# Strassen's seven block products in the output projection of an attention and SwiGLU kernel, with x in a ring of six batches

## The chip, the cores and the metric

The kernel runs on one core of a Trainium2 chip. The metric is device time in microseconds (us), the median of several runs; lower is better. The engines are TensorE (PE; its weight loads are shown as PEld), VectorE (DVE), ScalarE (ACT), GpSimd (POOL) and SyncE (SP, which issues DMAs here).

## What is computed

Attention with a decay per position, causal, for 8 batches of 8 heads with 576 positions of 64 numbers; its output, laid out as 4608 tokens of 512 numbers, goes through a SwiGLU block with a width of 1536. Inputs and output are float32.

```python
scores = scale * np.matmul(q, k.transpose(0, 1, 3, 2))
cum = np.cumsum(np.log(np.clip(f, 0.0001, 1.0)), axis=-1)
scores = np.where(causal, -1000000000.0, scores + cum[:, :, :, None] - cum[:, :, None, :])
attn = softmax(scores)                       # over the last axis
x = np.matmul(attn, v).transpose(0, 2, 1, 3).reshape(B * S, H * D)   # 4608 x 512
g = x @ w_gate                               # w_gate, w_val: 512 x 1536
out = (g * (1.0 / (1.0 + np.exp(-g))) * (x @ w_val)) @ w_out         # w_out: 1536 x 512
```

## The kernel before

All matrix products take bf16 operands and accumulate in float32 in PSUM, which is divided into eight banks of 128 x 512 float32: four in a pool "f" (the block's products), two in "s" (attention's scores), one in "o" (attention's output), one in "t" (transposes).

Attention goes by pairs of heads of a batch (`attention`, and `attention2` for batch 0). Scores (`score`, line 699) go to a bank, ACT takes the exponential (`expo`, line 733), POOL zeroes what is above the diagonal (`mask`, line 742), PE weighs the values (`weigh`, line 756), DVE divides by the sums (lines 763 and 768), and a transpose on PE or by DMA puts the result into `xT`, which holds x transposed for all 4608 tokens.

The block goes by nine tiles of 512 tokens (`ffn`). Twelve units per tile (`unit`), one for each 128 of the 1536 columns: PE computes the gate product in four matmuls (`gate`, line 901) into one bank and the value product into another; ACT takes tanh(g/2) (line 905), DVE adds 1 and multiplies by g (line 909), then by the value product (line 912), which gives twice the wanted result as a bf16 block in `HH` (16 buffers of 128 x 512). The output projection (`project`, line 916) then takes the tile in four blocks of 128 tokens: for each, twelve matmuls of 512 columns, with a block of `HH` as the weights and `wo` streaming, into one bank. ACT copies the bank to `OT` with a factor 0.5 (line 920), and SP stores 256 KB (line 923). For the very last block of tokens the 512 columns are cut at 256, 384 and 448.

The order of the instructions on each engine is fixed when the kernel is built. Operations are declared with a key, the operations they come after, the buffers that they take and a cost in us for each engine that may run them. A planner (`Plan.run`) simulates the engines with these costs: whenever an engine comes free, it issues the ready operation with the lowest key. Attention has keys from 1000 to some 9000, the block's PE work keys from 100000 up by tile, the block's ACT and DVE work -5 and -4. So on PE attention goes first whenever it is ready, and the block fills what is left. A table of keys for the first operations, `ORDER`, replaces their computed keys. On the chip each engine goes through its list in order and waits where an input is late.

Of the kernel before, what the change touches and what calls it, by code (L numbers as in the profile page):

```python
# [9 lines left out]
F32 = mybir.dt.float32  # L10
# [210 lines left out]
def kernel(ctx, tc, q, k, v, f, w_gate, w_val, w_out, out):  # L221
    nc = tc.nc
# [30 lines left out]
    def sb(name, shape, dt):  # L253
        return consts.tile(shape, dt, name=name)
# [23 lines left out]
    def ps(b):  # L278
        return bank[bank_of[b.pool] + b.i]
# [5 lines left out]
    flat = OT[1][:, :NFL]  # L285
    ones = OT[0].bitcast(BF16)[:BH, :S]
# [4 lines left out]
    zc, zt = HH[0][:, :384], HH[1][:, :384]  # L291
    QN = [[xT[:, r, c * S : (c + 2) * S].rearrange("p (u x) -> p u x", u=2) for r in range(KD)] for c in (6, 4)]

    plan = Plan(
        {"f": 4, "s": 2, "o": 1, "t": 1, "qk": NQK, "pt0": NPT0, "pt": NPT, "vb": NVB, "nv": NNV,
         "xn": NXN, "rc": NRC, "th": NTH, "hh": NHH, "ot": NOT},
        lambda t: 2.0 if t < TWARM else 1.0,
    )

# [21 lines left out]
    def copy(e, dst, src):  # L321
        if e == "ACT":
            nc.scalar.activation(dst, src, AF.Copy)
        else:
            E[e].tensor_copy(dst, src)  # L325
# [449 lines left out]
    def put(e, p, bt, qb, nq):  # L775
        b, r = divmod(p, FB)
        n = min(S, (qb + nq) * P) - qb * P
        copy(e, xT[:, r, b * S + qb * P : b * S + qb * P + n], ps(bt).bitcast(BF16)[:, :n])

    def cross(e, p, bx):  # L780

        b, r = divmod(p, FB)
        dst = xT[:, r, b * S : b * S + NB * P].rearrange("p (n t) -> p n t", t=P)
# [40 lines left out]
    def attention2(b, key, parts):  # L824

        bx = {}
        for n, (bks, qb, nq) in enumerate(parts):
            ahead = len(parts) > 1 and n == 0
            got = {}
            for jj in range(4):  # L830
# [21 lines left out]
                for u, h in enumerate(heads):  # L852
# [13 lines left out]
                    if len(prev) == 2:  # L866
                        x_out(b * FB + r, qb, nq, bx[n, r], prev, kk)

    def attention(p, key):
        b = p // FB  # L870
        bks, qb, nq = (0, 1, 2, 3), 0, NB
        bx, scaled = Buf("xn"), []
        for j in range(2):
            h = 2 * p + j
            bo, ws, x1 = Buf("o"), [], None
            for m, i in enumerate(bks):
                bs = Buf("s")
                a = op(("PE", mm(*[x[2] for x in BANKS[i]])), score, h, i, bs, after=q_ready[h] + [o_qkz], take=[bs], use=[hqk[p]],
                       key=key + 0.5 * j + 0.1 * i, tag=("s", h, i))
# [17 lines left out]
            nc.gpsimd.dma_start(out=t[:, :, lo:hi], in_=src[:, :, lo:hi])  # L897

    def gate(e, w, fc, t0, n, bf):
        for ko in range(KD):  # L900
            nc.tensor.matmul(ps(bf)[:, :n], w[:, ko, fc * P : (fc + 1) * P], xT[:, ko, t0 : t0 + n],  # L901
                             start=(ko == 0), stop=(ko == KD - 1))

    def tanh(e, n, bf, bt):
        nc.scalar.activation(TH[bt.i][:, :n], ps(bf)[:, :n], AF.Tanh, scale=0.5)  # L905
# [2 lines left out]
        t = TH[bt.i][:, :n]  # L908
        nc.vector.scalar_tensor_tensor(out=t, in0=t, scalar=1.0, in1=ps(bf)[:, :n], op0=ALU.add, op1=ALU.mult)  # L909

    def times(e, n, bf, bt, bh, lo):
        nc.vector.tensor_mul(HH[bh.i][:, lo : lo + n], TH[bt.i][:, :n], ps(bf)[:, :n])  # L912

    def project(e, hs, lo, m, bf, fcs, c):
        for fc in fcs:
            nc.tensor.matmul(ps(bf)[:m, c], HH[hs[fc].i][:, lo : lo + m], wo[:, fc, c],  # L916
                             start=(fc == 0), stop=(fc == KF - 1))

    def out_copy(e, m, bf, bo, c):
        nc.scalar.activation(OT[bo.i][:m, c], ps(bf)[:m, c], AF.Copy, scale=0.5)  # L920

    def store(e, t0, m, bo, c):
        E[e].dma_start(out=out[t0 : t0 + m, c], in_=OT[bo.i][:m, c])

    w_ready = {}
    last_gate = [None]

    def unit(t, fc, t0, n, hs, lo, kk, after):
        needs = [o for a, b, done in x_ready.values() if a < t0 + n and b > t0 for o in done]
        wr = [w_ready["g", fc // FCG], w_ready["v", fc // FCG]]  # L930
        bg, bv, bt = Buf("f"), Buf("f"), Buf("th")
        g = op(("PE", mm(*[n] * KD)), gate, wg, fc, t0, n, bg, after=needs + wr + after, take=[bg], key=kk, tag=("gp", t, fc))
# [3 lines left out]
        fresh = hs[fc] is None  # L936
        if fresh:
            hs[fc] = Buf("hh")
            hs[fc].first = None
        m = op(("DVE", dve(n)), times, n, bv, bt, hs[fc], lo, after=[a, b, hs[fc].first],  # L940
               take=[hs[fc]] if fresh else [], use=[bv, bt] + ([] if fresh else [hs[fc]]), key=-5, tag=("mul", t, fc))
        if fresh:
            hs[fc].first = m
        return g, m

    def ffn(t, t0, n):
        key, hs, ms = 1e5 * (t + 1), [None] * KF, []
# [7 lines left out]
        for m0 in range(0, n, P):  # L955
            m = min(P, n - m0)
            bo = Buf("ot")
            cuts = ENDS if t0 + m0 + m == N_TOK else [0, DM]
            for c in (slice(a, b) for a, b in zip(cuts, cuts[1:])):
                w, at = c.stop - c.start, m0 + c.start / DM  # L960
                bf = Buf("f")
                a = None
                for g in range(NCO):
                    fcs = range(g * FCO, (g + 1) * FCO)
                    a = op(("PE", mm(*[w] * FCO)), project, hs, m0, m, bf, fcs, c,
                           after=[m_ for fc in fcs for m_ in ms[fc]] + [w_ready["o", c] for c in range(NCO)] + [a],
                           take=[] if g else [bf], use=[hs[fc] for fc in fcs] + ([bf] if g else []),
                           key=key + 2000 + at + 0.01 * g, tag=("fo", t, m0))
                a = op(("ACT", act(w)), out_copy, m, bf, bo, c, after=[a] + (o_out2 + regrouped if t == 0 else []), take=[] if c.start else [bo],
                       use=[bf] + ([bo] if c.start else []), key=-4, tag=("ot", t, m0))  # L970
                last = len(cuts) > 2 and c.stop == DM
                op(("ACT", 0.45) if last else ("SP", 0.7), store, t0 + m0, m, bo, c, after=[a], use=[bo], key=-4, dma=w / DM, packet=90, tag=("out", t, m0))

    for g in range(2):
        four(g, -20 + 5 * g)
# [159 lines left out]
```

## Time and profile before

| | |
|---|---|
| median of 3 runs | 383.54 us (383.19 to 383.68) |
| span of the profiled execution, first to last instruction | 381.2 us |
| PE busy | 372.5 us (98%) |
| PEld busy | 208.4 us (55%) |
| DVE busy | 217.8 us (57%) |
| ACT busy | 213.1 us (56%) |
| POOL busy | 139.3 us (37%) |
| gate and value products, line 901 | 110.1 + 109.3 us busy |
| output projection, line 916 | 103.1 us busy |

The page gives no time of its own for the profiled execution besides its span; the runs' times include what surrounds the span. "Busy" is the time covered by an engine's recorded instructions; matmuls are pipelined and overlap one another in the record, so the time from the start of one group to that of the next tells more of PE than the duration of one instruction. In a group's row, the number before the bar is the count, then come its busy time, the mean duration in ns, and the idle time of the engine before it with what ended it. A row of stretches gives each engine's busy time in that stretch, with the number of instructions in brackets. A row of the timeline gives start and length, and in brackets the idle time before it.

### The profile page before, as it was taken

The numbers are of one execution on the slowest core, as the hardware profiler recorded it, in microseconds if no ns is written. First come the engines' busy times: TensorE is split into PE (matmuls) and PEld (weight loads), VectorE is DVE, ScalarE is ACT, GpSimd is POOL, SyncE is SP. The second block draws the span as 40 slices with busy tenths as digits, with TensorE's granted clock in tenths as the row PEclk, the third lists the DMA queues.
The fourth block names the chain that finished last, engine by engine and source line by source line (L and its number), as shares of the span: only waits on it lengthen the run. The fifth ranks groups of instructions, "written<-read, shape, count | busy, mean of one in ns | idle before, by whom it ended". The sixth has DMA issues, their size and how long they took to land.

```text
span 381.2 us, 8360 instructions
## 1 busy us (share of the span) xinstructions
PE 372.5 (98%) x3105; PEld 208.4 (55%) x3151; DVE 217.8 (57%) x456; ACT 213.1 (56%) x436; POOL 139.3 (37%) x368
## 2 busy tenths in 40 slices
PE   8899999999999999999999999999999999999996
PEld 5667656546555555545565456545664444444444
DVE  7878995377425771477327751586228815733850
ACT  7999745247647665646675467647773323323322
POOL 8897337117534454344353446603440000000000
PEclk9999999999999999999999999999999999999999
DMA  8999996996598788999499959993431011002003
GB/s 146 192 196 197 206 204 128 198 198 122 106 217 198 148 152 158 226 180 197 99 210 204 191 119 218 194 194 72 108 95 40 2 55 55 2 28 83 3 0 111
DMA packets 125319, 51.96 MB, mean 136 GB/s; under 512 B 112110, under 2 KB 119726, under 8 KB 124510
## 3 DMA queue, kind: packets, MB, share of 16 engines
q1 hardware_dynamic: 108782, 36.18, 45.0%
q0 software_dynamic: 16288, 15.14, 27.0%
q8 instruction: 24, 0.39, 0.4%
q14 instruction: 17, 0.14, 0.1%
q10 hardware_dynamic: 208, 0.11, 0.1%
HBM read 38.56 MB, written 17.07 MB: 146 GB/s over the span
## 4 chain that ended last, share of the span: by engine, by line
PE 94%; DMA 2%; ACT 1%; issue 1%; POOL 1%; DVE 0%; POOLq 0%
PE ps L901 48%; PE ps L916 24%; PE ps L699 10%; PE ps L756 8%; DMA xT<-in_k_dram 2%; PE ps L717 1%; ACT PT L733 1%; PE ps L773 1%; PE ps L574 0%; POOL xT L550 0%; PE ps L725 0%; PE ps L1004 0%; ACT PTa L733 0%; PE ps L558 0%; DVE QK L325 0%
## 5 line engine op out<-in xcount | busy, mean ns | idle before, releaser
L905 ACT ACTIVATE th<-ps 128x512 f32<-128x512 f32 (+1 forms) x112 | 65.0, 582 | 87.8 <-PE ps L901 85.3
L901 PE MATMUL ps<-xT,wv 128*128 128x512 bf16 (+1 forms) x435 | 110.1, 371 | 0.7
L909 DVE SCALAR_TENSOR_TENSOR th<-th,ps 128x512 f32<-128x512 f32 (+1 forms) x112 | 74.5, 666 | 63.2 <-ACT th L905 63.1
L901 PE MATMUL ps<-xT,wg 128*128 128x512 bf16 (+1 forms) x434 | 109.3, 371 | 0.6
L916 PE MATMUL ps<-wo,hh 128*128 128x512 bf16 (+3 forms) x449 | 103.1, 362 | 1.0
L733 ACT ACTIVATE PT<-ps 128x512 bf16<-128x512 f32 (+2 forms) x192 | 91.3, 510 | 15.3 <-PE ps L699 9.2
L912 DVE TENSOR_TENSOR hh<-th,ps 128x512 bf16<-128x512 f32 (+1 forms) x112 | 74.6, 667 | 12.4 <-PE ps L901 2.0
L742 POOL TENSOR_SCALAR_AFFINE_SELECT PT<-PT 128x128 bf16<-128x128 bf16 (+1 forms) x192 | 52.1, 276 | 59.1 <-ACT PT L733 53.1
L901 PEld LDWEIGHTS <-wg 128*128 128x128 bf16 x448 | 42.5, 97 | 41.5
L901 PEld LDWEIGHTS <-wv 128*128 128x128 bf16 x448 | 42.4, 97 | 41.4 <-issue 0.2
L699 PE MATMUL ps<-QK 68*128 68x256 bf16 (+4 forms) x392 | 64.7, 261 | 0.2
L916 PEld LDWEIGHTS <-hh 128*128 128x128 bf16 x468 | 41.4, 97 | 34.0
L742 POOL TENSOR_SCALAR_AFFINE_SELECT PTa<-PTa 128x256 bf16<-128x256 bf16 x64 | 25.9, 408 | 78.5 <-ACT PTa L733 76.9
L763 DVE RECIPROCAL rc<-ps 128x5 f32<-128x5 f32 (+2 forms) x68 | 12.9, 190 | 66.0 <-PE ps L756 65.9
L920 ACT ACTIVATE ot<-ps 128x512 f32<-128x512 f32 (+3 forms) x39 | 22.0, 565 | 45.9 <-PE ps L916 43.2
L756 PE MATMUL ps<-VB,PT 128*128 128x65 bf16 x768 | 44.4, 193 | 0.1
L756 PEld LDWEIGHTS <-PT 128*128 128x128 bf16 x768 | 36.3, 97 | 13.9 <-POOL PT L742 1.3
L699 PEld LDWEIGHTS <-QK 68*128 68x128 bf16 x392 | 31.3, 97 | 17.3 <-ACT PT L733 0.3
L733 ACT ACTIVATE PTa<-ps 128x384 bf16<-128x384 f32 x64 | 30.9, 487 | 13.5 <-PE ps L699 12.5
L768 DVE TENSOR_TENSOR xn<-ps,rc 128x320 bf16<-128x320 f32 (+2 forms) x72 | 32.4, 453 | 2.2
L325 POOL CAST VB<-natv 128x512 bf16<-128x512 f32 (+1 forms) x32 | 19.0, 614 | 6.4 <-DMA natv<-in_v_dram 6.3
L756 PEld LDWEIGHTS <-PTa 128*128 128x128 bf16 x192 | 13.1, 97 | 11.0 <-POOL PTa L742 0.4
(72 smaller groups left out, 159.0 us busy)
## 6 DMA issues: line engine op xcount, KB each, us to landing
out_dram<-ot SPq DMA_DIRECT2D x35, 256.0 KB
natv<-in_v_dram SPq DMA_DIRECT2D x25, 256.0 KB
qk_d<-in_q_dram POOLq DMA_DIRECT2D x24, 144.0 KB, 3.9
qk_d<-in_k_dram POOLq DMA_DIRECT2D x24, 144.0 KB, 4.5
wv<-in_moe_w_val_dram POOLq DMA_DIRECT2D x3, 512.0 KB, 11.1
wg<-in_moe_w_gate_dram POOLq DMA_DIRECT2D x3, 512.0 KB, 12.4
wo<-in_moe_w_out_dram POOLq DMA_DIRECT2D x4, 384.0 KB, 13.1
xT<-in_k_dram POOLq DMA_DIRECT2D x4, 288.0 KB, 8.3
```

Of the source, the lines that this page charges most:

```text
L325: E[e].tensor_copy(dst, src)
L699: nc.tensor.matmul(s[:, c : c + w], QK[:KR, hqk[p].i, 1, j * S + kt * P : j * S + (kt + 1) * P], QK[:KR, hqk[p].i, 0, j * S + q0 : j * S + ...
L733: nc.scalar.activation(place(h, i)[:, OFFS[i] : OFFS[i] + c], ps(bs)[:, :c], AF.Exp, scale=0.125)
L742: nc.gpsimd.affine_select(out=d, in_=d, pattern=pat, compare_op=ALU.is_ge, fill=0.0, base=0, channel_multiplier=-1,)
L756: nc.tensor.matmul(o[:, lo : lo + D + 1], pt[:, c : c + P], VB[hvb[b].i][:, kt, hb, : D + 1], start=first and n == 0, stop=last and n == l ...
L768: nc.vector.tensor_mul(XN[bx.i][:, qb : qb + nq, j], o, r)
L901: nc.tensor.matmul(ps(bf)[:, :n], w[:, ko, fc * P : (fc + 1) * P], xT[:, ko, t0 : t0 + n], start=(ko == 0), stop=(ko == KD - 1))
L905: nc.scalar.activation(TH[bt.i][:, :n], ps(bf)[:, :n], AF.Tanh, scale=0.5)
L909: nc.vector.scalar_tensor_tensor(out=t, in0=t, scalar=1.0, in1=ps(bf)[:, :n], op0=ALU.add, op1=ALU.mult)
L912: nc.vector.tensor_mul(HH[bh.i][:, lo : lo + n], TH[bt.i][:, :n], ps(bf)[:, :n])
L916: nc.tensor.matmul(ps(bf)[:m, c], HH[hs[fc].i][:, lo : lo + m], wo[:, fc, c], start=(fc == 0), stop=(fc == KF - 1))
L920: nc.scalar.activation(OT[bo.i][:m, c], ps(bf)[:m, c], AF.Copy, scale=0.5)
```

## The change

From tile 2 on, the projection of 512 tokens (A: 512 x 1536) by `w_out` (B: 1536 x 512) is done as a product of 2 x 2 blocks after Strassen. A's blocks are halves of the tokens by alternate groups of 128 columns; a pair of `HH` blocks lies now in one buffer, [128, 2, 512], of which there are seven. B's blocks are alternate groups of 128 rows by halves of the columns. Seven products take the place of eight; each goes over 256 tokens (two row blocks q of 128) x 768 x 256 columns, that is 2 x 6 matmuls of 256 columns.

The left factors that are sums of blocks are formed by DVE, three operations for each of the six pairs (`sums`), in six buffers `SU`. The right factors that are sums of blocks of `wo` are formed once by DVE (`blend`, five operations), two of them in place in `wo` after the projections of tiles 0 and 1, which go on as before (`simple`). For each q, M3 and M4 share a bank, M1, M6 and M7 another; M5 and M2 accumulate on M3 and M4 after ACT has copied these to `OT`. The remaining additions are made by POOL and DVE in `OT` and from the bank (`both`, `more`, `apart`, `close`). In the last tile the products are split into the first four and the last two pairs, DVE does all additions, and the last row block has M6 in a bank of its own and is stored in four pieces.

`xT` is now a ring of six batches (3456 tokens); batches 6 and 7 overwrite batches 0 and 1 after the gate products that read them, and a gate product that crosses the end is split. Scores on PE keep the order in which they are declared. From tile 7 on the block's products may take banks from all four pools. The factor 0.5 moves from the copy to DVE's multiplication.

```diff
-NQK, NPT0, NPT, NVB, NNV, NXN, NTH, NHH, NOT, NRC = 8, 6, 5, 3, 6, 4, 4, 16, 3, 4
+NQK, NPT0, NPT, NVB, NNV, NXN, NTH, NHH, NSU, NOT, NRC = 8, 6, 5, 3, 5, 4, 4, 7, 6, 2, 4
...
-    xT = sb("xT", [P, KD, N_TOK + D], BF16)
+    xT = sb("xT", [P, KD, RING * S + D], BF16)
...
+    HH = [sb(f"hh{i}", [P, 2, MT], BF16) for i in range(NHH)]
+    SU = [sb(f"su{i}", [P, 5, HALF], BF16) for i in range(NSU)]
+    OT = [sb(f"ot{i}", [P, 2, DM], F32) for i in range(NOT)]
+    wt = sb("wt", [P, 3, KF // 2, HALF], BF16)
...
+                a = op(("PE", mm(*[x[2] for x in BANKS[i]])), score, h, i, bs, after=q_ready[h] + [o_qkz], behind=last_score[-1:], take=[bs], use=[hqk[p]],
                        key=key + 0.5 * j + 0.1 * i, tag=("s", h, i))
+                last_score.append(a)
...
     def gate(e, w, fc, t0, n, bf):
+        lo = t0 % (RING * S)
+        cut = min(n, RING * S - lo)
         for ko in range(KD):
+            for a, b in ((0, cut), (cut, n)):
+                if a < b:
+                    at = (lo + a) % (RING * S)
+                    nc.tensor.matmul(ps(bf)[:, a:b], w[:, ko, fc * P : (fc + 1) * P], xT[:, ko, at : at + b - a],
+                                     start=ko == 0 and a == 0, stop=ko == KD - 1 and b == n)
...
+    def sums(e, n, bh, bu):
+        h, u = HH[bh.i], SU[bu.i]
+        if n == 0:
+            o, x, y, f = u[:, 0:2], h[:, 0].rearrange("p (a c) -> p a c", a=2), h[:, 1].rearrange("p (a c) -> p a c", a=2), ALU.add
+        elif n == 1:
+            o, x, y, f = u[:, 2:4], h[:, :, HALF:], h[:, :, :HALF], ALU.subtract
+        else:
+            o, x, y, f = u[:, 4], h[:, 0, :HALF], h[:, 1, HALF:], ALU.add
+        E[e].tensor_tensor(out=o, in0=x, in1=y, op=f)
+
+    def product(e, hs, us, m, q, bf, gs, opens):
+        left, right, c = {
+            1: (lambda g: SU[us[g].i][:, 4], T1, 0), 2: (lambda g: SU[us[g].i][:, 1], B11, 1),
+            3: (lambda g: HH[hs[g].i][:, 0, :HALF], T3, 0), 4: (lambda g: HH[hs[g].i][:, 1, HALF:], T4, 1),
+            5: (lambda g: SU[us[g].i][:, 0], B22, 0), 6: (lambda g: SU[us[g].i][:, 2], T6, 1),
+            7: (lambda g: SU[us[g].i][:, 3], T7, 0)}[m]
+        for g in gs:
+            nc.tensor.matmul(ps(bf)[:, c * HALF : (c + 1) * HALF], left(g)[:, q * P : (q + 1) * P], right[:, g],
+                             start=opens and g == 0, stop=g == KF // 2 - 1, skip_group_check=True)
...
+            m3 = mul(3, bz, [], 0, True)
+            m4 = mul(4, bz, [m3], 0.1)
+            m1 = mul(1, bx, [], 0.2, True)
+            m6 = mul(6, by, [m1], 0.3, last)
+            a = op(("ACT", act(2 * HALF)), mid_copy, bz, bo, after=[m4] + (o_out2 + regrouped if t == 0 else []), take=[bo], use=[bz], key=at, tag=("ot", t, q))
+            m5 = mul(5, bz, [a, m4], 0.4)
+            m2 = mul(2, bz, [a, m5], 0.5)
+            b = op({e: f(HALF) for e, f in (LAST_ON if end else BOTH_ON).items()}, both, bo, after=[a], use=[bo], key=at, tag=("both", t, q))
+            c = op(("DVE", dve(HALF)), more, bx, bo, after=[b, m6], use=[bx, bo], key=at, tag=("more", t, q))
+            d = op(("ACT", act(2 * HALF)), mid_copy, bz, bo, after=[b, m2], use=[bz, bo], key=at, tag=("ot", t, q))
+            if not last:
+                m7 = mul(7, bx, [c, m6], 0.6)
+                b = op({e: f(2 * HALF) for e, f in (LAST_ON if end else APART_ON).items()}, apart, bo, after=[c, d], use=[bo], key=at, tag=("apart", t, q))
+                c = op(("DVE", dve(2 * HALF)), close, bx, bo, after=[b, m7], use=[bx, bo], key=at, tag=("close", t, q))
...
+            m7 = mul(7, bx, [c, m6], 0.6)
+            op(("SP", 0.7), store, t0 + P, 0, bo, slice(HALF, DM), after=[d], use=[bo], key=at, dma=0.5, packet=90, tag=("out", t, q, 2))
+            ab = [op(("DVE", dve(HALF, False)), apart1, bo, a, after=[c, d], use=[bo], key=at, tag=("apart", t, q)) for a in (1, 0)]
+            c = op(("DVE", dve(HALF)), close1, by, bo, 1, after=[ab[0], m6], use=[by, bo], key=at, tag=("close", t, q))
...
+            c = op(("DVE", dve(HALF)), close1, bx, bo, 0, after=[ab[1], m7], use=[bx, bo], key=at, tag=("close", t, q))
+            op(("ACT", 0.45), store, t0 + P, 0, bo, slice(0, HALF), after=[c], use=[bo], key=at, dma=0.5, packet=90, tag=("out", t, q, 3))
...
+QUICK = 2
...
+def F_POOLS(t):
+    return ("f", "s", "o", "t") if t >= WIDE_AT else ("f",)
...
+WIDE_AT = 7
...
+SUM_ON = [{"DVE": fast}, {"DVE": fast}, {"DVE": fast}]
+BOTH_ON = {"POOL": pool2}
+APART_ON = {"POOL": pool2}
+BLEND_ON = {"DVE": fast}
+LAST_ON = {"DVE": slow}
...
-ENDS = [0, 256, 384, 448, 512]
+SUM_KEY = 50000
+BLEND_KEY = 40000
```

The sums have the key 50000 and the blends 40000, so that DVE takes them only when nothing with a lower key is ready.

More of the change, by code (lines that the diff above doesn't have):

```diff
@@ L909, in silu @@
         nc.vector.scalar_tensor_tensor(out=t, in0=t, scalar=1.0, in1=ps(bf)[:, :n], op0=ALU.add, op1=ALU.mult)
[L911 to L920, printed above, removed]
@@ new lines, in both, with more, apart1, close1 @@
+    def both(e, bo):
+        o = OT[bo.i]
+        E[e].tensor_tensor(out=o[:, 0, :HALF], in0=o[:, 0, HALF:], in1=o[:, 1, :HALF], op=ALU.add)
+    def more(e, bf, bo):
+        o = OT[bo.i]
+        nc.vector.tensor_tensor(out=o[:, 1, HALF:], in0=ps(bf)[:, :HALF], in1=o[:, 0, :HALF], op=ALU.add)
+    def apart1(e, bo, a):
+        o = OT[bo.i]
+        c = edges(bo)[:, a]
+        E[e].tensor_tensor(out=c, in0=c, in1=o[:, 1, :HALF] if a else o[:, 0, HALF:], op=ALU.subtract)
+    def close1(e, bf, bo, a):
+        c = edges(bo)[:, a]
+        nc.vector.tensor_tensor(out=c, in0=ps(bf)[:, a * HALF : (a + 1) * HALF], in1=c, op=ALU.add)
@@ L925, with apart, close, store @@
+    def apart(e, bo):
+        o = OT[bo.i].rearrange("p a (s d) -> p (a s) d", s=2)
+        E[e].tensor_tensor(out=edges(bo), in0=edges(bo), in1=o[:, 1:3], op=ALU.subtract)
+    def close(e, bf, bo):
+        nc.vector.tensor_tensor(out=edges(bo), in0=ps(bf).rearrange("p (a d) -> p a d", a=2), in1=edges(bo), op=ALU.add)
+    def store(e, t0, a, bo, c=slice(0, DM)):
+        E[e].dma_start(out=out[t0 : t0 + P, c], in_=OT[bo.i][:, a, c])
     w_ready = {}
     last_gate = [None]
+    tails = []
@@ L935, in unit @@
         a = op(("PE", mm(*[n] * KD)), gate, wv, fc, t0, n, bv, after=[g], take=[bv], key=kk + 1, tag=("vp", t, fc))
-        fresh = hs[fc] is None
+        m = op(("DVE", dve(n)), times, n, bv, bt, hs[p], r, lo, after=[a, b, hs[p].first],
+               use=[bv, bt, hs[p]], key=-5, tag=("mul", t, fc))
         if fresh:
[L938 to L943, printed above, removed]
+            hs[p].first = m
+        read.append((t0, t0 + n, [g, a]))
         return g, m
+    read = []
     def ffn(t, t0, n):
-        key, hs, ms = 1e5 * (t + 1), [None] * KF, []
+        key, hs, ms = 1e5 * (t + 1), [None] * (KF // 2), []
         for fc in range(KF):
@@ L954, in ffn, with simple @@
         last_gate[0] = lg
-        for m0 in range(0, n, P):
-            m = min(P, n - m0)
+        tails.append((t, t0, key, hs, ms))
+    plain = []
+    def simple(t, t0, key, hs, ms):
+        for q in range(2):
             bo = Buf("ot")
[L958 to L972, printed above, removed]
@@ L1000 @@
         ffn(t, t0, MT)
+    for r in tails[:QUICK]:
+        simple(*r)
+    ready = [w_ready["o", c] for c in range(NCO)]
+    blended = [op({e: f((KF // 2) * HALF) for e, f in (DVE_ONLY if n == 1 else BLEND_ON).items()}, blend, n, after=ready, key=BLEND_KEY + n, tag=("blend", n)) for n in range(3)]
+    blended += [op({e: f((KF // 2) * HALF) for e, f in BLEND_ON.items()}, blend, n, after=blended[:3] + plain, key=BLEND_KEY + n, tag=("blend", n)) for n in (3, 4)]
+    for r in tails[QUICK:]:
+        finish(*r, blended)
+    for a, b, done in x_ready.values():
+        for lo, hi, ops in read:
+            if lo < b - RING * S + D and hi > a - RING * S:
+                for o in done:
+                    o.after.extend(ops)
     def dummy(i):
```

104 lines of the change are left out of this document (88 added, 16 removed).

## The prediction

> **What bounds the kernel now.** I read the page first: busy times, the chain that ended last, the costliest groups.
>
> ```profile
> span 381.2 us, 8360 instructions
> PE 372.5 (98%) x3105; PEld 208.4 (55%) x3151; DVE 217.8 (57%) x456; ACT 213.1 (56%) x436; POOL 139.3 (37%) x368
> PEclk9999999999999999999999999999999999999999
> PE 94%; DMA 2%; ACT 1%; issue 1%; POOL 1%; DVE 0%; POOLq 0%
> PE ps L901 48%; PE ps L916 24%; PE ps L699 10%; PE ps L756 8%; DMA xT<-in_k_dram 2%; PE ps L717 1%; ACT PT L733 1%; PE ps L773 1%; PE ps L574 0%; POOL xT L550 0%; PE ps L725 0%; PE ps L1004 0%; ACT PTa L733 0%; PE ps L558 0%; DVE QK L325 0%
> ```
>
> The reader should see one thing: TensorE (PE) is busy from end to end at full clock, and the chain runs through it for 94%. Line 901 (gate and value products) is half of that, line 916 (the output projection) a quarter. So columns taken off PE are time gained, as long as what replaces them does not make PE wait. Next, the stretches, cut where the output projections begin and end.
>
> ```profile
> core 0: us, PE busy (x) PEld busy (x) DVE busy (x) ACT busy (x) POOL busy (x), PEclk, DMA share, GB/s
> 101.30:114.10 12.80, 12.75 (x110) 7.11 (x109) 3.01 (x8) 6.12 (x13) 6.04 (x17) 1.00 0.93 191
> 114.10:143.00 28.90, 28.63 (x234) 16.20 (x237) 19.55 (x36) 19.14 (x39) 13.43 (x36) 1.00 0.81 168
> 156.80:182.20 25.40, 25.24 (x182) 13.40 (x184) 17.48 (x31) 14.54 (x29) 10.57 (x27) 1.00 1.16 196
> 182.20:199.30 17.10, 16.94 (x171) 10.42 (x173) 4.61 (x12) 12.42 (x27) 8.02 (x25) 1.00 0.76 151
> 199.30:225.10 25.80, 25.59 (x176) 13.46 (x179) 18.68 (x32) 14.31 (x29) 10.34 (x26) 1.00 1.00 184
> 240.00:266.60 26.60, 26.38 (x213) 14.61 (x216) 19.43 (x36) 15.54 (x32) 8.83 (x25) 1.00 0.87 163
> 315.90:336.60 20.70, 20.59 (x95) 9.41 (x96) 15.29 (x23) 7.76 (x13) 0.00 (x0) 1.00 0.04 13
> 336.60:347.00 10.40, 10.35 (x49) 4.70 (x48) 1.20 (x2) 1.79 (x3) 0.00 (x0) 1.00 0.20 76
> ```
>
> A token tile is a gate stretch, in which VectorE (DVE) is busy for about 70% of the time, and a projection stretch, in which DVE is nearly idle. Until 285 us attention is mixed in; the last rows are without it. That DVE load matters, because the new work lands there.
>
> **What PE saves.** The durations in the groups overlap, so I take the pitch from the end of the kernel, where each ScalarE (ACT) copy starts as its product group ends.
>
> ```profile
> 367.54 10.61 PE L916 MATMUL ps<-wo,hh 128*128 128x512 bf16 x84
> 370.38 0.60 ACT L920 ACTIVATE ot<-ps 128x512 f32<-128x512 f32 x1 [2.90 <-PE ps L916]
> 372.96 0.60 ACT L920 ACTIVATE ot<-ps 128x512 f32<-128x512 f32 x1 [1.99 <-PE ps L916]
> 375.56 0.60 ACT L920 ACTIVATE ot<-ps 128x512 f32<-128x512 f32 x1 [1.99 <-PE ps L916]
> 376.87 0.39 ACT L920 ACTIVATE ot<-ps 128x256 f32<-128x256 f32 x1 [0.71 <-PE ps L916]
> 377.49 0.92 ACT L920 ACTIVATE ot<-ps 128x128 f32<-128x128 f32 x3 [0.23 <-PE ps L916]
> 378.44 0.38 ACTq L923 DMA_DIRECT2D out_dram<-ot  x1
> ```
>
> Twelve matmuls of 512 columns end 2.59 us apart (372.96 to 375.56 is 2.60; 370.38 to 372.96 is 2.58), 0.2155 each; twelve of 256 take 1.31 us (375.56 to 376.87), 0.109 each. Two halves cost 0.003 us more than a whole, each with its own weight load: small matmuls lose nothing here. A tile now needs 48 of 512 columns, 10.34 us. Strassen needs seven products of 2 x 6 matmuls of 256 columns: 84 x 0.109 = 9.17 us. Saved: 1.17 us a tile, 7.0 us for tiles 2 to 7 (counted from 0). The last tile's 84 matmuls, in narrowing cuts, took 10.61 us; 84 at 0.109 save 1.44. **Total on PE: -8.46 us.** It counts in full only while PE has work at every moment.
>
> **The ring of x.** Tile 6 (tokens 3072 to 3583) wraps the ring of 3456 columns; its 96 gate matmuls are split 384 and 128, so 96 more instructions at 0.003: **+0.29 us**. Batches 6 and 7 overwrite batches 0 and 1, which tiles 0 to 2 read; tile 2's gates are over by 143 us, long before batch 6 is attended, so that wait is over before it begins: 0. Tiles 0 and 1 keep their 96 wide matmuls; the first batch's queries and keys are staged in the SU buffers instead of x, which nothing else uses that early; attention's scores are now kept in their listed order on PE, which waits for little there now (rival 3 has the row): 0 each.
>
> **The VectorE work.** Rows by form:
>
> ```profile
> L912 DVE TENSOR_TENSOR hh<-th,ps 128x512 bf16<-128x512 f32 x104 | 71.3, 687 | 11.7 <-PE ps L901 2.0 <-DVE th L909 0.5
> L909 DVE SCALAR_TENSOR_TENSOR th<-th,ps 128x256 f32<-128x256 f32 x8 | 3.4, 419 | 1.1 <-ACT th L905 1.0
> L325 DVE COPY xT<-ps 128x576 bf16<-128x576 bf16 x5 | 2.3, 457 | 4.0 <-PE ps L773 4.0
> L325 DVE COPY xT<-ps 128x256 bf16<-128x256 bf16 x4 | 1.2, 288 | 0.8 <-PE ps L773 0.8
> L325 POOL CAST VB<-natv 128x512 bf16<-128x512 f32 x25 | 15.1, 615 | 6.3 <-DMA natv<-in_v_dram 6.3
> L742 POOL TENSOR_SCALAR_AFFINE_SELECT PT<-PT 128x128 bf16<-128x128 bf16 x128 | 37.3, 294 | 39.8 <-ACT PT L733 35.4
> 355.42 0.69 DVE L909 SCALAR_TENSOR_TENSOR th<-th,ps 128x512 f32<-128x512 f32 x1 [0.25 <-ACT th L905]
> 355.45 1.03 PE L901 MATMUL ps<-xT,wg 128*128 128x512 bf16 x4
> 356.21 0.69 DVE L912 TENSOR_TENSOR hh<-th,ps 128x512 bf16<-128x512 f32 x1
> 357.14 0.69 DVE L909 SCALAR_TENSOR_TENSOR th<-th,ps 128x512 f32<-128x512 f32 x1 [0.25 <-ACT th L905]
> 367.50 0.69 DVE L909 SCALAR_TENSOR_TENSOR th<-th,ps 128x512 f32<-128x512 f32 x1 [0.25 <-ACT th L905]
> 368.30 0.69 DVE L912 TENSOR_TENSOR hh<-th,ps 128x512 bf16<-128x512 f32 x1
> ```
>
> Each Strassen tile adds 18 sums (6 pairs; 512, 512 and 256 elements, bf16). No such instruction is in the trace. Bounds: as slow as float work of that size, 0.687, 0.687 and 0.419, 10.8 us a tile; or at the rate of the bf16 copies, 0.288 for 256 and, between 0.288 and 0.457, 0.42 for 512: 1.13 a pair, 6.8 us a tile. I take 6.8, the rows with the same types. The Trainium skill, page "VectorE: DVE Perf Modes", section "The perf-mode tier table (the rule you actually need)", gives bf16 tensor_tensor in SBUF two elements a cycle; by the formula of its errata section a sum of 512 would be about 0.33 us, an estimate, 5.1 us a tile, and by it the stalls below would vanish and the sum would be 376.9. No row here shows it.
>
> A unit (one gate and one value product) comes every 1.72 us (355.42 to 357.14), of which DVE idles 0.25. In 315.9 to 336.6 us DVE has 20.7 - 15.3 = 5.4 us free. So 6.8 us of sums overrun a bare gate stretch by 1.4 us: about that much is late when the gates are done. That is the stall to price.
>
> After the last gate matmul (367.54) the last multiplication ends 1.45 us later (368.99). The last pair's sums add 1.13, the backlog 1.4: M1 and the others made from sums can be complete at +4.0. PE's cover meanwhile: in the last tile the first parts of M3, M4, M1 and M6, 32 matmuls, 3.5 us: stall 0.5. At tiles 6 and 7 the cover is M3 and M4 of both row blocks (24 matmuls, 2.6 us) and two units of the next tile (3.45), 6.1 us in all, since seven HH pairs allow no more; those units bring DVE 2 x 1.48 us, so the sums end at +6.9 and PE waits 0.8 each. Tiles 2 to 5 have attention as further cover (the projection stretch 182.2 to 199.3 lasts 17.1, of which 10.3 is projection): 0, and up to 1 us each if the static order puts M1 ahead of it. **Sum of stalls: +2.1 us**, from 0 (sums at the faster rate) to the second rival.
>
> The five blends (1536 elements: about 0.96 us by the copies' slope of 0.53 ns an element, the negating one 1.75 in the float rate, 5.6 us in all) run once. Tile 1's projection stretch has 9.8 us of idle DVE and tile 2's products come 29 us later: 0. Without that cover, 5.6.
>
> **The added waits.** Within a row block M5 waits for ACT's copy of M3 and M4 (0.60, plus about 0.1), behind M1 and M6 (1.31): hidden unless ACT is two exponentials late. All later PE work queues behind M5. M7 waits for DVE's addition, that for POOL's, that for the copy: 0.1 + 0.6 + 0.1 + POOL 0.3 to 1.2 (0.615 for one input of 512; half for the size, up to double for two inputs) + 0.1 + 0.42, about 1.9, against four products, 2.6. Behind POOL's addition queue attention's masks and behind them PE's line 756; behind DVE's stand the next units, which have about 1.1 us to spare: with four PSUM banks a value bank is wanted again 1.72 + 0.86 us after its unit ended, and is free after 1.45. I take 0. ACT's copies stay four of 0.60 a tile; stores stay two a row block on SP, a little later, with the two double OT buffers refilled only 30 us on: 0.
>
> **The end.** Now the last store is issued 0.29 us after PE's end (378.15 to 378.44). Then: M2 ends 0.65 before PE does; ACT's copy 0.1 + 0.60; then four DVE operations of 256 at 0.42 and 0.1, so the store comes 1.8 us after PE's end: **+1.5 us** (0.2 if only the last operation is late, 2 if DVE is).
>
> **Sum.** -8.46 + 0.29 + 2.1 + 1.5 = -4.6 us. The page gives the span, 381.2; the median of the three runs, 383.54, lies 2.3 us above, for what surrounds the span, which stays. Span 376.6; time **379.0 us**.
>
> **Rivals.**
> (1) All sums are covered: no stalls, 383.54 - 6.7 = 376.9, or 375.6 with the end at its lower bound. For it: DVE is at 57%, and with 7 x (6.8 + 2 x 1.1) + 5.6 = 69 us more at 76% of the new span. Against: the gate stretches, where its slack is 5 us.
> (2) DVE becomes the bound, and the kernel slower. From the last sum of one tile, PE does the ten products made from sums (6.55), restarts gates, DVE follows 1.7 us later (355.45 to 357.14) and needs 10 x 1.48 for the units and S for the sums: 23.0 + S, against PE's 29.9 a tile. It decides from S = 6.9 us; every us above costs one in each of tiles 6, 7 and 8. At the float bound (10.8) that is 3.9 x 3 = 11.7, and in the attention stretches DVE would have 17.5 + 10.8 = 28.3 in 25.4 us, partly covered, say 2 more: 376.9 + 13.7 = 390.6. It passes 383.5 from S = 9.1, that is 0.5 us a sum. For it: my S of 6.8 stands right at the edge, and dependent DVE operations leave 0.1 us between them. Against: the bf16 copies.
> (3) Sums and masks exclude each other. In the four attention gate stretches POOL is busy for 43 of 107 us, 40%; of 72 sums 29 would meet a POOL instruction, and if each delays a mask, and with it PE, by half a mask (0.15), that is 4.3 us: 383.3. The Trainium skill, page "SBUF — State Buffer", section "Who interferes with whom", says a VectorE instruction with two SBUF inputs contends with a GpSimd instruction that reads SBUF, the later one blocked for the whole of the earlier; VectorE's present operations mostly have one input in PSUM, so no run here shows it. Against it as a loss of time: masks end few of PE's waits now.
>
> ```profile
> PEld L756 <- POOL PT L742: 1.3, 6, 0.3
> ```
>
>
> **Chances.** Forecast, with 0 to 5 us of stalls (376.9 to 381.9): 0.54. Rival 1: 0.14. Rival 3: 0.12, of which 0.04 is faster by over 0.2%, 0.05 the same, 0.03 slower. Rival 2: 0.20. A measurement can tell about 0.2%, 0.77 us, from no change: faster 0.53 + 0.14 + 0.04 = 0.71 (0.01 of the forecast, with every stall at its worst, counts as the same); same 0.01 + 0.05 = 0.06; slower 0.20 + 0.03 = 0.23. The range runs from rival 1's lower bound, 375.6, to 386.0, inside rival 2; what lies beyond is most of rival 2 (0.16). The forecast's own range is 376.9 to 381.9.
>
> **What would show it.** Right: matmuls of the products at 84 a tile, 0.65 us for six; PE's waits in tiles 6 to 8 on the sums, near 2 us together; last PE matmul to last store 1.8 us; sums of 512 near 0.42. Wrong: sums near 0.69 with PE waiting at every boundary (rival 2), waits of line 756 on longer masks (rival 3), PE waiting for ACT's copies or POOL's additions, or M5 and M7 being the late ones.

## The result: 1% slower

| | before | changed |
|---|---|---|
| time, median of 5 runs each | 383.19 us (382.54 to 383.68) | 387.70 us (385.07 to 388.11) |
| ratio | | 1.0101, 95% interval 1.0072 to 1.0131 |
| span of the profiled execution | 381.2 us | 386.4 us (its time: 388.11) |
| end of the last matmul | 378.15 us | 381.97 us |

The prediction was 379.0 us. The changed kernel's page, its busy row, clock and chain:

```profile
span 386.4 us, 9163 instructions
PE 370.2 (96%) x3430; PEld 237.6 (61%) x3463; DVE 278.3 (72%) x620; ACT 212.5 (55%) x434; POOL 166.5 (43%) x392
PEclk9999999899999999999999999999999999999998
DVE 5%; PE 2%; issue 1%; POOLq 0%; DVEq 0%; ACT 0%
PE ps L959 2%; DVE hh L926 2%; DVE th L923 2%; DVE su L950 1%; POOLq L1307 0%; DVE ot L999 0%; ACT ot L972 0%; DVEq L1307 0%; DVE ot L988 0%; DVEq L926 0%; DVE ot L992 0%
```

PE is no longer busy to the end, its clock has a dent, and the chain, followed back over the last 35 us before it is lost, runs mostly through VectorE. The groups:

```profile
L950 DVE TENSOR_TENSOR su<-hh 128x512 bf16<-128x512 bf16 x84 | 35.1, 447 | 0.9
L950 DVE TENSOR_TENSOR su<-hh 128x256 bf16<-128x256 bf16 x42 | 13.5, 322 | 0.0
L936 DVE SCALAR_TENSOR_TENSOR wt<-wo 128x1536 bf16<-128x1536 bf16 x1 | 4.1, 4068 | 0.0
L979 POOL TENSOR_TENSOR ot<-ot 128x256 f32<-128x256 f32 x12 | 8.7, 726 | 47.9 <-ACT ot L972 47.9
L746 POOL TENSOR_SCALAR_AFFINE_SELECT PT<-PT 128x128 bf16<-128x128 bf16 x128 | 39.0, 307 | 34.6 <-ACT PT L737 31.1
```

The sums are of the size that I took. One instruction stands out: the negating blend, once, 4.07 us where I had put 1.75. The longest of PE's waits, apart from those of the first 16 us, which come to 3.2 us here and 2.6 before:

```profile
PE ps L760 <- DVE xn L772: 2.3, 5, 0.6
PE ps L966 <- DVE hh L926: 1.4, 1, 1.4
PE ps L760 <- POOL PT L746: 0.9, 2, 0.5
PE ps L959 <- DVE su L950: 0.4, 1, 0.4
```

Most of it is neither the products (959) waiting for sums nor M5 and M7 waiting for copies. It is attention's line 760, waiting for VectorE's division (772), and the plain projection of tile 0 (966). VectorE, POOL and PE around the latter, from the timeline:

```profile
59.99 2.27 POOL L329 CAST VB<-natv 128x512 bf16<-128x512 f32 x4
60.01 4.07 DVE L936 SCALAR_TENSOR_TENSOR wt<-wo 128x1536 bf16<-128x1536 bf16 x1
62.73 1.82 POOL L329 CAST VB<-natv 64x512 bf16<-64x512 f32 x1
64.00 0.68 DVE L923 SCALAR_TENSOR_TENSOR th<-th,ps 128x512 f32<-128x512 f32 x1
64.78 0.69 DVE L926 SCALAR_TENSOR_TENSOR hh<-th,ps 128x512 bf16<-128x512 f32 x1
65.53 0.39 PE L966 MATMUL ps<-wo,hh 128*128 128x512 bf16 x1 [1.37 <-DVE hh L926]
66.52 0.32 PE L760 MATMUL ps<-VB,PTa 128*128 128x65 bf16 x3 [0.60 <-DVE xn L772]
```

For 4 us nothing else passes VectorE; tile 0's last unit waits behind it, and PE for that unit. Stretches of the same kernel:

```profile
core 0: us, PE busy (x) PEld busy (x) DVE busy (x) ACT busy (x) POOL busy (x), PEclk, DMA share, GB/s
64.00:66.00 2.00, 0.55 (x2) 0.11 (x2) 1.86 (x6) 0.05 (x1) 1.94 (x4) 1.00 1.19 237
66.00:68.00 2.00, 1.48 (x17) 1.08 (x17) 1.76 (x4) 0.55 (x1) 0.00 (x0) 0.61 1.29 227
68.00:70.00 2.00, 2.00 (x6) 0.71 (x5) 0.26 (x1) 0.00 (x0) 0.00 (x0) 0.54 0.43 141
118.50:148.20 29.70, 28.30 (x231) 15.72 (x232) 26.80 (x52) 18.72 (x40) 14.52 (x36) 1.00 0.90 168
243.40:270.30 26.90, 26.25 (x208) 14.40 (x210) 24.23 (x51) 15.16 (x31) 11.09 (x30) 1.00 0.91 180
322.00:343.20 21.20, 20.89 (x94) 9.27 (x95) 18.38 (x36) 7.17 (x13) 1.27 (x1) 1.00 0.09 33
```

PE's pause is followed by a granted clock of 0.61 and 0.54, so the pause is paid for again: (1 - 0.61) x 2 + (1 - 0.54) x 2 = 1.7 us. The mean granted clocks of the five runs fit this: 0.992 to 0.994 in the three of 387.7 us and more, 0.997 in those of 385.1 and 385.7. Only the slowest of the five was profiled, so that the others differ by this dip is not shown; in c_price, below, the clock dips in the first 15 us instead. In the attention gate stretches VectorE is now busy for 90% (26.80 of 29.70, 24.23 of 26.90). What that does to PE, near 130 us:

```profile
129.45 1.72 DVE L950 TENSOR_TENSOR su<-hh 128x512 bf16<-128x512 bf16 x3
131.09 0.18 DVE L767 RECIPROCAL rc<-ps 128x5 f32<-128x5 f32 x1
131.31 0.49 DVE L772 TENSOR_TENSOR xn<-ps,rc 128x320 bf16<-128x320 f32 x1
131.85 0.25 PE L760 MATMUL ps<-VB,PTa 128*128 128x65 bf16 x3 [0.54 <-DVE xn L772]
```

Three sums in a row (1.72 us where 0.42 + 0.42 + 0.28 would do; POOL masks and converts at that time) stand ahead of a division, and attention's only output bank is free when the division is done. Over the whole kernel the sums took 4.0 us more of VectorE than at 0.42 and 0.28 us each (84 at 0.447 and 42 at 0.322 on average).

### The profile page after: what moved, and what is told of

Same layout as the page of the kernel before. It is cut to its first block, busy times and chain, and to the rows that moved or that the text cites. A ratio compares the mean times of both kernels' runs of the same rounds, so it can differ in the third digit from the quotient of the medians.

```text
span 386.4 us, 9163 instructions
## 1 busy us (share of the span) xinstructions
PE 370.2 (96%) x3430; PEld 237.6 (61%) x3463; DVE 278.3 (72%) x620; ACT 212.5 (55%) x434; POOL 166.5 (43%) x392
## 5 line engine op out<-in xcount | busy, mean ns | idle before, releaser
L915 PE MATMUL ps<-xT,wv 128*128 128x512 bf16 (+2 forms) x484 | 109.9, 350 | 1.0 <-DVE th L923 0.2
L915 PE MATMUL ps<-xT,wg 128*128 128x512 bf16 (+2 forms) x478 | 109.2, 350 | 1.2
L737 ACT ACTIVATE PT<-ps 128x384 bf16<-128x384 f32 (+2 forms) x192 | 91.3, 510 | 16.7 <-PE ps L703 8.8
L926 DVE SCALAR_TENSOR_TENSOR hh<-th,ps 128x512 bf16<-128x512 f32 (+1 forms) x112 | 74.3, 668 | 11.5 <-PE ps L915 0.9
L703 PE MATMUL ps<-QK 68*128 68x256 bf16 x392 | 63.7, 261 | 0.1
L950 DVE TENSOR_TENSOR su<-hh 128x512 bf16<-128x512 bf16 (+1 forms) x126 | 47.0, 405 | 0.9
L959 PEld LDWEIGHTS <-su 128*128 128x128 bf16 x420 | 39.8, 97 | 6.6 <-DVE su L950 1.0
L760 PEld LDWEIGHTS <-PT 128*128 128x128 bf16 x768 | 35.1, 98 | 9.0 <-POOL PT L746 1.1
L959 PE MATMUL ps<-wt,su 128*128 128x256 bf16 x252 | 33.6, 272 | 0.7 <-DVE su L950 0.4
L972 ACT ACTIVATE ot<-ps 128x512 f32<-128x512 f32 x28 | 16.7, 598 | 28.8 <-PE ps L959 27.5
L979 POOL TENSOR_TENSOR ot<-ot 128x256 f32<-128x256 f32 x12 | 8.7, 726 | 47.9 <-ACT ot L972 47.9
## 6 DMA issues: line engine op xcount, KB each, us to landing
wo<-in_moe_w_out_dram POOLq DMA_DIRECT2D x4, 384.0 KB, 13.5
```

Of the source, the lines that this page charges most:

```text
L703: nc.tensor.matmul(s[:, c : c + w], QK[:KR, hqk[p].i, 1, j * S + kt * P : j * S + (kt + 1) * P], QK[:KR, hqk[p].i, 0, j * S + q0 : j * S + ...
L737: nc.scalar.activation(place(h, i)[:, OFFS[i] : OFFS[i] + c], ps(bs)[:, :c], AF.Exp, scale=0.125)
L760: nc.tensor.matmul(o[:, lo : lo + D + 1], pt[:, c : c + P], VB[hvb[b].i][:, kt, hb, : D + 1], start=first and n == 0, stop=last and n == l ...
L915: nc.tensor.matmul(ps(bf)[:, a:b], w[:, ko, fc * P : (fc + 1) * P], xT[:, ko, at : at + b - a], start=ko == 0 and a == 0, stop=ko == KD - ...
L926: nc.vector.scalar_tensor_tensor(out=HH[bh.i][:, r, lo : lo + n], in0=TH[bt.i][:, :n], scalar=0.5, in1=ps(bf)[:, :n], op0=ALU.mult, op1=AL ...
L950: E[e].tensor_tensor(out=o, in0=x, in1=y, op=f)
```

## Experiments

Theory A was that three losses on VectorE, each in its place, ate the gain; rival B that the rebuilt frame (ring, seven pairs, order of scores) costs by itself. Times are medians beside runs of the kernel before on the same chip, whose medians were 383.4 to 383.5.

**b_late.** The first three blends wait for tile 1's first projection block.

```diff
-    blended = [op({e: f((KF // 2) * HALF) for e, f in (DVE_ONLY if n == 1 else BLEND_ON).items()}, blend, n, after=ready, key=BLEND_KEY + n, tag=("blend", n)) for n in range(3)]
+    blended = [op({e: f((KF // 2) * HALF) for e, f in (DVE_ONLY if n == 1 else BLEND_ON).items()}, blend, n, after=ready + plain[4:5], key=BLEND_KEY + n, tag=("blend", n)) for n in range(3)]
```

> The first three blends are formed after tile 1's first projection block instead of as soon as the output weights are there. Theory A (losses of the changed kernel: one blend that holds VectorE for 4 us at 60 us, 4.4 us of PE with the half clock that follows; 4.4 us of waits in the attention stretches; 2.9 us in the last three tiles; 2.2 us after PE's end): the stall at 63.8 us and the half clock after it go, 387.7 to about 383.5 us. Rival B (the loss is in the rebuilt frame: ring, seven HH pairs, kept order of the scores): about 387. If the blend only blocks another stretch: 386 to 388, with a stall near 110 us.

Measured 383.89 us, ratio to before 1.001 (0.9994 to 1.0026): 3.8 us less than the changed kernel, or 3.5 by the two ratios. In its timeline:

```profile
104.71 1.75 DVE L936 SCALAR_TENSOR_TENSOR wt<-wo 128x1536 bf16<-128x1536 bf16 x1
106.38 0.95 DVE L940 TENSOR_TENSOR wt<-wo 128x1536 bf16<-128x1536 bf16 x1
106.53 1.07 POOL L746 TENSOR_SCALAR_AFFINE_SELECT PTa<-PTa 128x256 bf16<-128x256 bf16 x1 [2.29 <-ACT PTa L737]
107.65 0.26 PE L760 MATMUL ps<-VB,PTa 128*128 128x65 bf16 x3 [0.47 <-POOL PTa L746]
```

Undisturbed, the negating blend takes the 1.75 us that I had put. The wait at 64 us and the dip of the clock are gone: three blends in a bad place, by the trace above all the negating one, made the difference between no change and slower. The next blend still meets a mask, holds it up to 1.07 us (0.42 is usual) and costs PE 0.47, my third rival in small.

**b_nosums.** As b_late; products take blocks of `HH` where they took sums, and the sums are left out.

```diff
-            for n in range(3):
+            for n in range(0):
...
-            1: (lambda g: SU[us[g].i][:, 4], T1, 0), 2: (lambda g: SU[us[g].i][:, 1], B11, 1),
+            1: (lambda g: HH[hs[g].i][:, 0, :HALF], T1, 0), 2: (lambda g: HH[hs[g].i][:, 0, HALF:], B11, 1),
...
```

> As b_late, and the 18 sums a tile are left out: the products that take sums of blocks of the left factor take one of its blocks instead, so the output is not the reference's. Theory A (VectorE's queue, filled with the sums, makes PE wait): waits in the attention stretches and the last tiles go too, about 377.5 us (376.9 and what is left of the end). Rival B: 383 or more. Rival C (the waits come from the chain of copies and additions around M5 and M7, not from the sums): 382 to 383, PE still waiting in the product stretches.

Measured 378.33 us, ratio 0.9876 (0.9858 to 0.9894). The sums cost 5.6 us (383.89 - 378.33). The two profiled executions differ by 5.8 us, of which 0.85 lies ahead of tile 2's first tanh (117.27 and 116.42 us), before any sum, so by the traces the sums cost some 5 us. Without them PE has no wait of over 0.2 us after 270 us; M5, M7 and the additions, which stay, hold up nothing of note: rival C is out, and rival B too.

**b_two_out.** As b_late, with a second output bank for attention.

```diff
-            bo, ws, x1 = Buf("o"), [], None
+            bo, ws, x1 = Buf(*(("o", "t") if p >= 3 * FB else ("o",))), [], None
```

> As b_late, and attention's output may take the transposes' bank too from pair 12 on, so that a new head need not wait until VectorE has emptied the one bank. Theory A1 (PE waits because one bank is emptied late): PE's waits before line 760, some 3.5 us after 120 us, go: about 380. Theory A2 (VectorE has too much to do in these stretches, and PE waits for it in another place): about 383.5 like b_late, the waits turning up before line 915.

Measured 382.86 us, ratio 0.9984 (0.9968 to 1.0): 1.0 us less than b_late, under a third of what theory A1 gave. PE's waits, of b_late first:

```profile
PE ps L760 <- DVE xn L772: 1.2, 3, 0.5
PE ps L760 <- POOL PTa L746: 0.5, 1, 0.5
PE ps L760 <- POOL PT L746: 0.5, 1, 0.5
```

and of b_two_out:

```profile
PE ps L959 <- DVE hh L926: 0.7, 2, 0.5
PE ps L760 <- POOL PTa L746: 0.5, 1, 0.5
```

The division ends no wait of PE any more; a product waits for a unit instead. Both A1 and A2 were half right. The profiled execution was this kernel's fastest, 381.49 us, so its waits may be fewer than usual.

**plain9.** No Strassen in any tile; the frame stays.

```diff
-QUICK = 2
+QUICK = 9
...
```

> No Strassen: all nine tiles are projected the plain way, no blends, no sums; ring, seven HH pairs and order of scores stay. Theory A: like the kernel before, 383.5 (the ring's split costs 0.3, the last block is no longer cut, 0.5 more at the end): 383 to 384.5. Rival B: 387, for the frame itself costs.

Measured 384.44 us, ratio 1.0027 (1.0013 to 1.004). The frame costs 1.0 us, not the 3.5 of rival B. So in b_late Strassen wins 0.5 us at most, and the two intervals overlap, where some 8 were cut from PE.

**c_silu.** As b_two_out, with one VectorE operation a unit less in tiles 7 and 8.

```diff
+    def silu1(e, n, bf, bt):
+        nc.scalar.activation(TH[bt.i][:, :n], ps(bf)[:, :n], AF.Silu)
+    def times1(e, n, bf, bt, bh, r, lo):
+        nc.vector.tensor_tensor(out=HH[bh.i][:, r, lo : lo + n], in0=TH[bt.i][:, :n], in1=ps(bf)[:, :n], op=ALU.mult)
...
```

> As b_two_out (382.9 us), and in tiles 7 and 8 ScalarE computes g times its sigmoid itself, so that VectorE has one multiplication a unit instead of two operations. Theory D (in the last tiles VectorE is the bound: 3.65 us for two units with their sums against PE's 3.45): PE's waits after 320 us, about 1.9, go, and VectorE's work ahead of the last additions with them: about 381.0. Rival E (the waits there come from PSUM banks or from the order of M1 to M7): 382.9.

Measured 381.36 us, ratio 0.9946 (0.9926 to 0.9965): 1.5 us less than b_two_out, the expected 1.9 but for 0.4. In its profile PE waits for nothing after 320 us. It does wait 1.9 us at 248 us, for values that POOL converts late because they landed late; b_two_out's profile has no such wait. Theory D holds: in the changed kernel's last tile, two units with their sums take VectorE 3.66 us, PE 3.45:

```profile
365.76 0.68 DVE L923 SCALAR_TENSOR_TENSOR th<-th,ps 128x512 f32<-128x512 f32 x1
366.55 0.69 DVE L926 SCALAR_TENSOR_TENSOR hh<-th,ps 128x512 bf16<-128x512 f32 x1
367.15 0.62 DVE L950 TENSOR_TENSOR su<-hh 128x256 bf16<-128x256 bf16 x2
367.69 0.68 DVE L923 SCALAR_TENSOR_TENSOR th<-th,ps 128x512 f32<-128x512 f32 x1
368.48 0.69 DVE L926 SCALAR_TENSOR_TENSOR hh<-th,ps 128x512 bf16<-128x512 f32 x1
369.08 0.42 DVE L950 TENSOR_TENSOR su<-hh 128x512 bf16<-128x512 bf16 x1
369.42 0.68 DVE L923 SCALAR_TENSOR_TENSOR th<-th,ps 128x512 f32<-128x512 f32 x1
```

**c_price.** As b_two_out, with the planner's price of the unit's multiplication raised.

```diff
-        m = op(("DVE", dve(n)), times, n, bv, bt, hs[p], r, lo, after=[a, b, hs[p].first],
+        m = op(("DVE", dve(n) + (0.1 if t >= QUICK else 0)), times, n, bv, bt, hs[p], r, lo, after=[a, b, hs[p].first],
```

> As b_two_out, and from tile 2 on the planner is told that VectorE's second operation of a unit takes 0.1 us longer, which is the wait for the first one that the trace shows and the planner leaves out. Theory F (the static order is wrong because the planner thinks VectorE faster than it is): PE gets other work where it now waits, 1 to 2 us less, about 381.5. Theory D (VectorE's capacity is the bound): no change, 382.5 to 383.3.

Measured 381.24 us, ratio 0.9932 (0.9908 to 0.9957): 1.6 us less than b_two_out, no work changed. The planner puts the multiplication (0.61 us by its formula) straight behind the first operation; on the chip it starts 0.11 later than that ends (365.76 + 0.68 to 366.55). Told so, it orders PE's list differently. Theory F holds, and against my alternative both F and D are true: by the medians, capacity and order each cost about 1.5 us. How often the late values of 248 us strike each of these kernels is not known; such a wait is as large as these differences. In c_price's profiled execution it is absent, and the granted clock is 0.85 and 0.81 from 5 to 10 and 10 to 15 us.

**c_last_plain.** As b_two_out; tile 8 projected the plain way, its last block cut in four.

```diff
...
-    for r in tails[QUICK:]:
+    for r in tails[QUICK:8]:
         finish(*r, blended)
+    restored += [op(("DVE", fast((KF // 2) * HALF)), restore, n, after=halves, key=BLEND_KEY + 9 + n, tag=("restore", n)) for n in range(2)]
+    for r in tails[8:]:
+        simple(*r)
...
```

> As b_two_out, and the last tile is projected the plain way with its last block cut in four as before; two extra VectorE operations give back the two blocks of the weights that were overwritten. Lost: 1.4 us of PE columns. Won, if my account of the end is right: 0.9 us of waits for the last sums and 2 us after PE's end: 381.4. If the longer end of the changed kernel is not from its chain of additions: 384.

Measured 382.59 us, ratio 0.9974 (0.9954 to 0.9993), 0.3 less than b_two_out instead of 1.5. The end came as expected: from PE's last matmul to the span's end it takes 2.7 us (378.68 to 381.4), in c_price 4.5 (374.99 to 379.5). But PE still waits 0.4 and 0.2 us at the end of tile 7, and in the profiled run 1.9 us at 248 us for values that landed late, as in c_silu; whether this is in all runs stays open.

**c_tail_plain.** The same from tile 6 on (`tails[QUICK:6]`, `tails[6:]`).

> As c_last_plain, with tiles 6 and 7 plain too, so that Strassen serves tiles 2 to 5 alone, where attention is mixed in. Against c_last_plain it gives up 2.3 us of columns and wins back the waits at the ends of tiles 6 and 7 (some 1.2): 382.5. If Strassen in these tiles costs more than it saves: below c_last_plain.

Measured 383.10 us, ratio 0.998 (0.9961 to 0.9999), 0.5 more than c_last_plain, where 1.1 was expected: if this stands, Strassen in tiles 6 and 7 saves 2.3 us of columns and keeps 0.5. The two intervals overlap almost wholly, so it is not shown.

**d_tt.** The changed kernel, its blend as a plain addition.

```diff
-            nc.vector.scalar_tensor_tensor(out=T7, in0=B21, scalar=-1.0, in1=B22, op0=ALU.mult, op1=ALU.subtract)
+            nc.vector.tensor_tensor(out=T7, in0=B21, in1=B22, op=ALU.add)
```

> The changed kernel with its blend T7 as a tensor_tensor addition (1.75 us when undisturbed becomes 0.95), planned at the old price so that the order stays; its sign is wrong, and so is the output. Theory G (the 4.07 us are 2.3 us of waiting for POOL's conversions of values and 1.75 of work, since only one of the two engines gets at the second operand): about 2.3 + 0.95 = 3.2 us, and POOL's last conversion is held up for about 1 us in place of 1.8. Rival H (that form of VectorE instruction is slow by itself): 0.95 us, and PE's wait at 64 us is gone.

A single run, 385.85 us. Its timeline:

```profile
60.40 2.28 POOL L329 CAST VB<-natv 128x512 bf16<-128x512 f32 x4
60.41 3.28 DVE L936 TENSOR_TENSOR wt<-wo 128x1536 bf16<-128x1536 bf16 x1
63.14 1.02 POOL L329 CAST VB<-natv 64x512 bf16<-64x512 f32 x1
```

3.28 us against 3.2 by theory G and 0.95 by rival H; the conversion behind it is held up to 1.02 instead of 1.82, by as much as the blend's own work is shorter. The two engines exclude each other: each waits while the other works, and VectorE waited for four conversions in a row. PE's pauses were 0.58 and 0.60 us here, and the granted clock stayed at 1.00 from 60 to 70 us.

**e_best.** b_late, b_two_out, c_price and c_silu together.

> All remedies together: blends late, two output banks, the planner's price, ScalarE's own sigmoid product in tiles 7 and 8. If each took away a loss of its own (c_price and c_silu 1.5 us each below b_two_out's 382.9), about 379.8 us, faster than before by 0.9%, with PE waiting less than 1 us after 100 us. If price and ScalarE's product mend the same waits: 381.

Measured 379.99 us, ratio 0.991 (0.9892 to 0.9927), 2.9 us less than b_two_out: by the medians the two 1.5 us add up. The profiles leave it open: from tile 2's first tanh to PE's last matmul, b_two_out took 258.6 us, c_price 257.5 and e_best 256.9.

**e_pace.** e_best with `PACE = 8.6`.

> As e_best, and attention's inputs are planned 8.6 us apart instead of 8.8, so that they are loaded earlier. Two of the last profiles show PE waiting 2 us near 248 us for values that landed late. If late loads are now a steady cost, 379.0; if that wait was chance, 379.8 like e_best, or a little more for attention crowding the earlier tiles.

Measured 383.07 us, ratio 0.9988 (0.9972 to 1.0004): 3.1 us more than e_best. Earlier loads pull attention into tile 2: from its first tanh to tile 3's it takes 48.2 us, in e_best 41.7. PE's waits between 115 and 195 us come to 2.1 us, in e_best to 0.2, and from 162.0 to 165.4 us the granted clock is 0.50, another 1.7 us. In e_best's profile PE does not wait at 248 us; how steady that wait is, this run can't tell. The spacing is a tuned value.

**e_all.** e_best with tile 8 plain and cut.

> As e_best, with the last tile plain and cut. Lost: 1.4 us of columns; won: 1.8 us after PE's end: 379.4, at most 0.4 us below e_best. If the last tile's waits were already gone, e_best and this are the same.

Measured 379.59 us, ratio 0.990 (0.9884 to 0.9916). It is 1% faster than the kernel before; e_best it beats by less than the runs can tell. Its page has PE busy for 369.5 of 377.6 us (98%).

## Why the prediction was wrong

**The columns, right.** The pitch of 0.109 held to the end. The end of the last row block, from the changed kernel's timeline:

```profile
379.71 1.47 PE L959 MATMUL ps<-wo,su 128*128 128x256 bf16 x12
381.16 0.81 PE L959 MATMUL ps<-wt,su 128*128 128x256 bf16 x6
381.22 0.60 ACT L972 ACTIVATE ot<-ps 128x512 f32<-128x512 f32 x1 [1.56 <-PE ps L959]
381.85 0.76 DVE L988 TENSOR_TENSOR ot<-ot 128x256 f32<-128x256 f32 x2 [0.74 <-ACT ot L972]
382.53 0.75 DVE L992 TENSOR_TENSOR ot<-ps,ot 128x256 f32<-128x256 f32 x2
383.31 0.38 ACTq L1002 DMA_DIRECT2D out_dram<-ot  x1
```

Two products, M5 and M2, start 1.45 us before the next one (379.71 to 381.16): twelve at 0.109, and a wait of 0.14. **The end, right in size:** +1.5 predicted, and the store is issued 1.34 us after PE's end instead of 0.29, with 0.3 more until the span ends. **Sums and copies, right in size:** 0.42 and 0.28 undisturbed, POOL's additions 0.73 inside the 0.3 to 1.2, and the waits of M5 and M7 hidden but for this 0.14, as b_nosums shows.

**The blends, "0": the first step that failed.** It measured 3.8 us (387.70 - 383.89): 1.4 and 0.6 us of waits and 1.7 us of clock in the profiled execution. I placed them in tile 1's idle projection stretch; nothing in the code puts them there. They are ready when the weights are, and the planner gave them VectorE at 57 and 60 us, in tile 0's gates, beside POOL's conversions of values. I had also priced the blend as if alone, while my third rival said how it would not be. The Trainium skill, page "SBUF — State Buffer", section "Who interferes with whom", states that VectorE with two SBUF inputs and GpSimd reading SBUF block each other for whole instructions. The trace agrees, at 4.07 (2.3 of waiting and 1.75 of work) and 3.28 (2.3 and 0.95). I applied it to masks alone, and left the clock out: a PE pause cost 1.7 us again. The Trainium skill's page "TensorE: Matmul & The Clock Gate", section "Part 1: The HAM clock gate (the "warmup" mystery)", has half clock after an idle window of some 3.4 us. Here two pauses of 1.4 and 0.6 us with one matmul between them were followed by it; in e_pace pauses of up to 0.52 us were, in c_silu one of 1.9 us and in d_tt the two of 0.6 us were not. What decides it, these runs don't show.

**The attention stretches, "0, and up to 1 us each": the second.** I let attention be cover for PE and did not count it as load on VectorE, although my own row said 19.55 of 28.90 us; with sums it is 26.80 of 29.70. And the one output bank makes attention itself wait for VectorE. From tile 2's first tanh to tile 6's, b_late takes 167.23 us (117.27 to 284.50) and b_nosums 164.82 (116.42 to 281.24): the sums cost 2.4 us here, inside the four times 1 us that I allowed, but 0 in my sum. Whether it is their load on VectorE or its waits for POOL (most of the 4.0 us above) is not separated.

**The last tiles, 2.1 us, about right, by luck.** From tile 6's first tanh to PE's last matmul, b_late takes 93.53 us (284.50 to 378.03) and b_nosums 90.86 (281.24 to 372.10): the sums cost 2.7 us. With one VectorE operation less a unit in tiles 7 and 8, c_silu takes 90.80 (284.48 to 375.28). But it was not where I put it: PE lost it in small steps during the gates, as VectorE took 3.66 us for 3.45, which is 1.3 us over a tile's six pairs, and less at the products. Two errors cancelled in my overrun of 1.4 us. The rows from 365.76 on show that back to back a pair's sums take 0.88 us (0.54 + 0.34), so 5.3 a tile and not 6.8. They also show that a unit takes VectorE 1.39 us, 0.11 of it a wait between its two operations, so that a bare gate stretch has 4.0 us free (20.7 - 12 x 1.39) and not 5.4.

**Together:** -8.46 + 0.29 + 1.5 (columns, wrap, end) would be 376.9. The blends add 3.8, the sums 5.6, and 1.4 stays unassigned (b_nosums' 378.33 - 376.9), 0.5 of it the blend that meets a mask at 106 us: 387.7. These are differences of medians taken at different times; by the ratios to the kernel before, the blends are 3.5. Rival 2 named the engine, but not the way: S was 6.9 us a tile by recorded durations ((35.1 + 13.5) / 7), just its point, yet only 5.3 back to back; a bare gate stretch is bound by VectorE, a tile as a whole is not. Rival 3 had the mechanism and the wrong victim: the masks of 128 x 128 took 0.307 us on average instead of 0.294, and it was mostly the sums, a blend and a conversion that waited.

## What to carry to other kernels

Before work is moved to an engine that is idle on average, ask of each stretch what else stands in that engine's list there, and who waits behind it; a long instruction that is wanted late still blocks the list from the moment it is issued. An operand layout change (here two SBUF inputs) can tie two engines that were independent. A price that left out 0.1 us of a dependent operation was worth about 1.6 us in this planner's order, as much as taking work away.

## What the runs showed of the hardware

A VectorE instruction with two inputs in SBUF and POOL's conversions exclude each other: 1.75 us of work took 4.07, 0.95 took 3.28, and a conversion of 0.6 us took 1.82. After pauses of PE of 1.4 and 0.6 us the granted clock was 0.61 and 0.54 over the next four microseconds; in e_pace it was 0.50 for 3.4 us; after a pause of 1.9 us in c_silu it stayed at 1.00. A multiplication on VectorE that needs the operation before it started 0.11 us after that one's end (365.76 + 0.68 to 366.55); a sum of 512 that needs nothing new let the next operation start 0.34 us after its own start, though it is recorded with 0.42 (369.08 to 369.42).
